# Moving the attention denominators of a four-layer block: eleven under x^T k, five under the outputs, and key sums in half rows

## The chip, the cores and the metric

The kernel runs on one core of one Trainium2 chip. The metric is the device time of one execution in microseconds (us), as the median of several executions. A step of 2% would be 33 us; everything below is about single microseconds, so the argument rests on the traces, in which stretches repeat to 0.01 us, and the medians only confirm it. Blocks marked as profile show chosen lines of a view; "..." marks lines left out (in the prediction's blocks they are left out without a mark).

## The reference

Four layers with residuals: linear attention (A), a gated feed-forward (B), A, B, on x of 2048 x 1024.

```python
def _A_ref(x, wqkv, wo):                 # 32 heads of 32
    ...                                  # q, k, v from x @ wqkv
    phi = lambda t: jnp.where(t > 0, t + 1, jnp.exp(t)) + 1e-6
    pq, pk = phi(q), phi(k)
    kv  = jnp.einsum("bhsd,bhse->bhde", pk, v)
    z   = jnp.einsum("bhsd->bhd", pk)                      # the key sum
    num = jnp.einsum("bhqd,bhde->bhqe", pq, kv)
    den = jnp.einsum("bhqd,bhd->bhq", pq, z)[..., None] + 1e-6   # the denominators
    o = num / den
    return (...o...) @ wo

x = x + _A_ref(_layernorm(x), A_wqkv, A_wo)
x = x + _B_ref(_layernorm(x), B_W_gate, B_W_up, B_W_down)
...                                      # and both once more
```

## The kernel before

The kernel works in 16 blocks of 128 rows, in four quarters of four blocks. In an attention layer TensorE first projects k and q with phi on the other engines, then forms x^T k for the whole sequence (the "x^T k phase", 16 units of 16 matmuls), then projects the last quarter of q, folds kv into the output weights (16 fold matmuls), and computes the outputs. TensorE writes each result into a buffer of its accumulator memory, PSUM, and can reuse the buffer only when VectorE or ScalarE has read it; copying a result out is called its evacuation. The denominators, one per block and head, must be applied to the phi of q before its transpose goes to the outputs. Three parts per block: a product on GpSimd, a sum and a reciprocal on VectorE, a scaling on GpSimd; then a transposing DMA.

```python
def z_mult(sc, j):
    prod = self.prodp.tile([P, D], F32, tag="prod")        # one buffer
    nc.gpsimd.tensor_tensor(out=prod, in0=pq_of[sc, j], in1=zrow, op=ALU.mult)
    later.at(2, lambda: z_sum(prod, sc, j))

def z_sum(prod, sc, j):
    den = self.small.tile([P, D // HD], F32, tag="den")
    nc.vector.tensor_reduce(out=den, in_=heads(prod), ...)
    nc.vector.tensor_scalar(out=den, in0=den, scalar1=1e-6, ...)
    nc.vector.reciprocal(out=den, in_=den)
    later.at(2, lambda: z_scale(den, sc, j))

def z_scale(den, sc, j):
    nc.gpsimd.tensor_tensor(out=heads(pq), in0=heads(pq), in1=den..., op=ALU.mult)
    ...
    nc.sync.dma_start_transpose(out=pqT[sc][:, :, j * P:(j + 1) * P], in_=pq)
```

`later.at(n, f)` calls f after n further steps; a step is one unit of eight matmuls. It places an instruction in the program of its engine. The engines themselves are only held by the semaphores of the data. In the order in which they stand in the source: the phi of one unit on ScalarE and VectorE, the evacuation of a fold, and the schedule.

```python
nc.scalar.activation(out=e, in_=ps, func=ACT.Exp)                     # phi, form "v"
nc.vector.tensor_scalar(out=e, in0=e, scalar1=1.0, scalar2=1e-6,      # L305
                        op0=ALU.min, op1=ALU.add)
nc.vector.scalar_tensor_tensor(out=out, in0=ps, scalar=0.0, in1=e,    # L316
                               op0=ALU.max, op1=ALU.add)
...
if g % 2:                                                             # a fold's PSUM tile
    nc.scalar.activation(out=dst, in_=ps, func=ACT.Copy)
else:
    nc.vector.tensor_copy(out=dst, in_=ps)                            # L466
...
later.at(ZR, z_row)                                # the key sum, spread over all partitions
for i in range(self.ST - QT):
    later.at(ZR + 2 + i * 5 // 2, lambda i=i: z_mult(*divmod(i, QT)))
for d in range(KT):
    m_units(d)                                     # the x^T k phase
...
run(q3[:3])                                        # last quarter's q, then with folds
run([with_fold(u, i) for i, u in enumerate(q3[3:] + out0[:3])])
...
for j in range(QT):
    later.at(1 + Z3 * j, lambda j=j: z_mult(self.NQ - 1, j))
run(out0[3:])
```

Of the kernel before, what the change touches and what calls it, by code (L numbers as in the profile page):

```python
# [7 lines left out]
ALU = mybir.AluOpType  # L8
# [5 lines left out]
NW = 512  # L14
HD = 32
QT = 4
LNLAG = 1
ZR = 5
Z3 = 3
PHILAG = 2  # L20
KINDS = (("vvss", "vvss"), ("vvss", "vvss"))
# [62 lines left out]
class _Net:  # L84
# [255 lines left out]
    def layer_A(self, l, last_ln):  # L340
        nc, G, KT, D = self.nc, self.G, self.KT, self.D
        ring, later = self.ring, self.later
        H = D // NW
# [5 lines left out]
        ksum = self.prodp.tile([P, D], F32, tag="prod", name=f"ksum{l}")  # L349

        def project(name, l_q, j):
            w = ring.get((l, name))
            ps = self.ps.tile([P, NW], F32, tag="a")
            for kt in range(KT):
                nc.tensor.matmul(ps, lhsT=self.xnT[l, l_q][:, kt, j * P:(j + 1) * P],  # L355
                                 rhs=w[:, kt, :], start=(kt == 0), stop=(kt == KT - 1))
            return ps

        def k_unit(q, j, c):
            t = q * QT + j  # L360
            pk = self.pk_home(l, t)
            self.phi(project(f"k{c}", q, j), pk[:, c * NW:(c + 1) * NW], KINDS[l // 2][min(q, 1)][c])
            if c == H - 1:
                later.at(1 + self.phi_lag, lambda: k_sum(t))

        def k_sum(t):
            pk = self.pk_home(l, t)
            if t == 0:
                nc.gpsimd.tensor_copy(out=ksum, in_=pk)  # L369
            else:  # L370
                nc.gpsimd.tensor_tensor(out=ksum, in0=ksum, in1=pk, op=ALU.add)  # L371

        def z_row():

# [9 lines left out]
        def m_units(d):  # L384
            mt = self.ep.tile([P, D], BF16, tag="e", name=f"mt{l}_{d}")
            for h in range(H):
                ps = self.ps3.tile([P, NW], F32, tag="b")
                for t in range(self.ST):
                    nc.tensor.matmul(ps, lhsT=self.xn[l, t][:, d * P:(d + 1) * P],  # L389
                                     rhs=self.pk[l, t][:, h * NW:(h + 1) * NW],  # L390
                                     start=(t == 0), stop=(t == self.ST - 1))
                    if t == self.ST // 2 - 1:
                        later.tick()
                nc.scalar.activation(out=mt[:, h * NW:(h + 1) * NW], in_=ps, func=ACT.Copy)
                if h == H - 1:
                    later.at(2, lambda: kv_step(d, mt))
                later.tick()
# [35 lines left out]
        def z_mult(sc, j):  # L433
            prod = self.prodp.tile([P, D], F32, tag="prod")
# [5 lines that stand above are left out]
            nc.vector.tensor_reduce(out=den, in_=heads(prod), axis=mybir.AxisListType.X, op=ALU.add)  # L440
            nc.vector.tensor_scalar(out=den, in0=den, scalar1=1e-6, scalar2=None, op0=ALU.add)
            nc.vector.reciprocal(out=den, in_=den)  # L442
            later.at(2, lambda: z_scale(den, sc, j))
# [10 lines left out]
        def fold_wo(i):  # L454
            n2, g = divmod(i, G)
            if n2 == 0 and g % 2 == 0:
                T.append(self.slab.tile([P, 2, D], BF16, tag="slab", name=f"T{l}_{g // 2}"))
            pool, tag = (self.kvp, f"kv{g // 2 % 2}") if g % 2 else (self.ps3, "b")
            ps = pool.tile([P, NW], F32, tag=tag, name=f"fold{l}_{i}")
            nc.tensor.matmul(ps, lhsT=kvT[:, g, :], rhs=ring.get((l, f"o{n2}"))[:, g, :],  # L460
                             start=True, stop=True)
            dst = T[g // 2][:, g % 2, n2 * NW:(n2 + 1) * NW]
            if g % 2:
# [3 lines that stand above are left out]
# [16 lines left out]
        def column_major(f, q):  # L483
            return [lambda j=j, c=c: f(q, j, c) for c in range(H) for j in range(QT)]

        def row_major(f, q):
            return [lambda j=j, c=c: f(q, j, c) for j in range(QT) for c in range(H)]

        def run(*lists):

            n = max(len(u) for u in lists)
            for i in range(n):
                for u in lists:
                    if i < len(u):
                        u[i]()
                        later.tick()
# [5 lines left out]
        for i in range(QT, self.ST):  # L502
            self.ln_at((4 if l == 0 else 2) + 3 * (i - QT), l, i, 2)
        first = column_major(k_unit, 0)
        if l == 0:

# [16 lines left out]
        for q in range(1, self.NQ - 1):  # L523
            run(row_major(k_unit, q), row_major(q_unit, q))
        run(row_major(k_unit, self.NQ - 1))
        with self.tc.manual_schedule(engines={mybir.EngineType.DVE, mybir.EngineType.Pool}):
            ring.free_before((l, "v0"))
            later.at(ZR, z_row)
            for i in range(self.ST - QT):
                later.at(ZR + 2 + i * 5 // 2, lambda i=i: z_mult(*divmod(i, QT)))  # L530
            for d in range(KT):
                m_units(d)
            if l > 0:
                later.at(1, lambda: [self.bring_back(t) for t in range(self.NS)])
            q3 = row_major(q_unit, self.NQ - 1)
            out0 = column_major(out_unit, 0)

            def with_fold(u, i):
                return lambda: (u(), fold_wo(2 * i), fold_wo(2 * i + 1))

            run(q3[:3])
            run([with_fold(u, i) for i, u in enumerate(q3[3:] + out0[:3])])
            ring.free_slowly((l, "o0"), later, 2)
            for j in range(QT):
                later.at(1 + Z3 * j, lambda j=j: z_mult(self.NQ - 1, j))
            run(out0[3:])
            self.ln_later(last_ln, 0, 5, 4, 3)
            for sc in range(1, self.NQ):
                run(row_major(out_unit, sc))
# [132 lines left out]
```

## Time and profile before

The kernel before took 1641.26 us (median of the runs). Its trace, from the starts of TensorE's instructions in the timeline:

| stretch | us | of it lost |
|---|---|---|
| fourth group of transposes to the first x^T k matmul, first layer (17.94 to 109.37) | 91.43 | 1.8 |
| first last-quarter matmul to the next layer, first attention layer (168.18 to 244.15) | 75.97 | 3.0 |
| the same, second attention layer (979.82 to 1055.78) | 75.96 | 3.0 |

The prediction read the ends of the last stretch from another view, each 0.16 later; the length is the same. I shall call the first stretch the *first quarter* (its waits all lie there) and the others the *fold stretch*. The lines of the page, of the waits and of the fold stretch are in the prediction. For the first quarter, these are lines of VectorE and GpSimd from the timeline (start, length, line, operation, tiles, shapes; in brackets what the engine waited for):

```profile
21.13 0.85 DVE L305 TENSOR_SCALAR e<-e 128x512 f32<-128x512 f32 x1 [0.53 <-ACT e L304]
...
26.83 2.03 DVE L305 TENSOR_SCALAR e<-e 128x512 f32<-128x512 f32 x1 [0.53 <-ACT e L304]
28.78 0.68 DVE L316 SCALAR_TENSOR_TENSOR slab<-ps,e 128x512 bf16<-128x512 f32 x1
...
20.67 1.04 POOL L369 CAST ksum<-slab 128x1024 f32<-128x1024 bf16 x1 [19.36 <-DVE slab L316]
24.13 4.44 POOL L371 TENSOR_TENSOR ksum<-ksum,slab 128x1024 f32<-128x1024 f32 x2 [2.42 <-DVE slab L316]
```

Two whole-row key sums stand back to back from 24.13 on; the L305 that starts at 26.83 ends only 0.3 us after them, and the L316 behind it frees the PSUM buffer that TensorE waits for until 29.51. The first sum, at 20.67, stretches the L305 of 21.13 to 0.85.

### The profile page before, as it was taken

How to read it: one execution, taken by the hardware profiler on the slowest of the kernel's cores; microseconds unless marked ns; L12 is line 12 of the kernel's file. 1: busy time of each engine (PE TensorE's matmuls, PEld its weight loads, DVE VectorE, ACT ScalarE, POOL GpSimd, SP SyncE). 2: the span in 40 equal slices, each digit the busy share in tenths (PEclk: the TensorE clock that was granted, in tenths of full speed). 3: DMA queues.
4: the chain of work that ended last, by engine and by line, in shares of the span. 5: the costliest groups of instructions: out<-in, count | busy, mean ns of one | idle time of the engine just before them, and what ended most of it. 6: DMA issues, size and time to landing. Idle time of an engine off the chain costs nothing.

```text
span 1639.1 us, 18247 instructions
## 1 busy us (share of the span) xinstructions
PE 1617.8 (99%) x7506; PEld 742.7 (45%) x7658; DVE 576.8 (35%) x947; ACT 332.6 (20%) x635; POOL 194.7 (12%) x102
## 2 busy tenths in 40 slices
PE   8999999999999999999999999999999999999999
PEld 3444444444444444444444444444444444444444
DVE  7854686122212321222165548842121112211111
ACT  5741202101110110111067312121011101101110
POOL 1249220000000000000023574100000000000000
PEclk9999999999999999999999999999999999999999
DMA  8313537458445544544550148374544464455442
GB/s 252 57 52 59 173 65 177 149 167 238 155 138 171 179 151 158 160 151 138 168 129 1 58 102 237 72 199 145 176 150 150 158 197 153 141 162 161 155 160 71
DMA packets 298244, 235.04 MB, mean 143 GB/s; under 512 B 101296, under 2 KB 294192, under 8 KB 298160
## 3 DMA queue, kind: packets, MB, share of 16 engines
q1 hardware_dynamic: 293408, 229.66, 47.5%
q10 hardware_dynamic: 4752, 4.20, 0.8%
q8 instruction: 60, 0.98, 0.3%
q14 instruction: 24, 0.20, 0.0%
HBM read 201.33 MB, written 8.39 MB: 128 GB/s over the span
## 4 chain that ended last, share of the span: by engine, by line
PE 83%; DVE 1%; issue 1%; ACT 0%; ACTq 0%
PE acc L605 23%; PE pu L581 23%; PE pg L581 23%; PE ps L355 6%; PE ps L389 3%; PE ps L472 3%; PE acc_last L605 0%; DVE e L305 0%; PE kv L402 0%; DVE T L466 0%; DVE den L440 0%; DVE pq L316 0%; PE fold L460 0%; DVE kvT L414 0%; DVE den L442 0%
## 5 line engine op out<-in xcount | busy, mean ns | idle before, releaser
L581 PEld LDWEIGHTS <-t 128*128 128x128 bf16 x3584 | 350.7, 98 | 422.8
L581 PE MATMUL pu<-xnT,t 128*128 128x512 bf16 x1757 | 420.2, 379 | 1.9
L581 PE MATMUL pg<-xnT,t 128*128 128x512 bf16 x1756 | 419.8, 379 | 1.8
L605 PE MATMUL acc<-t,hT 128*128 128x512 bf16 x1727 | 380.6, 379 | 1.9
L587 DVE TENSOR_TENSOR hT<-pu,rg 128x512 bf16<-128x512 f32 x224 | 154.7, 691 | 572.7 <-PE pu L581 553.3
L586 ACT ACTIVATE rg<-pg 128x512 f32<-128x512 f32 x224 | 133.5, 596 | 737.0 <-PE pg L581 665.5
L605 PEld LDWEIGHTS <-hT 128*128 128x128 bf16 x1820 | 178.1, 98 | 209.0
L355 PE MATMUL ps<-t,xnT 128*128 128x512 bf16 x1002 | 223.0, 379 | 4.2 <-DVE slab L316 1.3
L355 PEld LDWEIGHTS <-xnT 128*128 128x128 bf16 x1024 | 99.8, 98 | 123.5 <-issue 3.2
L472 PE MATMUL ps<-T,pqT 128*128 128x512 bf16 x502 | 111.6, 379 | 1.1 <-DVE T L466 0.6
L154 ACT ACTIVATE rstd<-mv,eps 128x1 f32<-128x1 f32 x64 | 18.8, 294 | 332.4 <-DVE mv L152 332.4
L622 DVE TENSOR_TENSOR xo<-x,acc 128x512 bf16<-128x512 f32 x31 | 21.3, 687 | 170.3 <-PE acc L605 170.3
L147 DVE BATCH_NORM_STATS2 stats<-x 128x6 f32<-128x512 f32 (+1 forms) x120 | 78.1, 672 | 0.8
L472 PEld LDWEIGHTS <-pqT 128*128 128x128 bf16 x512 | 50.1, 98 | 61.3 <-issue 1.1
L435 POOL TENSOR_TENSOR prod<-pq,zrow 128x1024 f32<-128x1024 bf16 x32 | 68.3, 2134 | 72.0 <-DVE den L440 61.2
L369 POOL CAST ksum<-x 128x1024 f32<-128x1024 bf16 x1 | 1.0, 1037 | 621.5 <-DVE x L316 621.5
L619 DVE TENSOR_TENSOR x<-x,acc 128x512 f32<-128x512 f32 x32 | 21.6, 674 | 138.5 <-PE acc L605 137.4
L316 DVE SCALAR_TENSOR_TENSOR pq<-ps,e 128x512 bf16<-128x512 f32 x64 | 43.9, 687 | 57.9 <-ACT e L311 57.3
L447 POOL TENSOR_TENSOR pq<-pq,den 128x1024 bf16<-128x1024 bf16 x32 | 61.5, 1923 | 13.0 <-DVE den L442 13.0
L371 POOL TENSOR_TENSOR ksum<-ksum,slab 128x1024 f32<-128x1024 f32 x23 | 49.2, 2140 | 86.8 <-DVE slab L316 76.8
L305 DVE TENSOR_SCALAR e<-e 128x512 f32<-128x512 f32 x80 | 49.2, 615 | 28.5 <-ACT e L304 28.4
L440 DVE TENSOR_REDUCE den<-prod 128x32 f32<-128x1024 f32 x32 | 38.9, 1216 | 49.9 <-POOL prod L435 49.9
(58 smaller groups left out, 619.5 us busy)
## 6 DMA issues: line engine op xcount, KB each, us to landing
t<-in_B_W_gate_dram SPq DMA_DIRECT2D x56, 1024.0 KB, 6.7
t<-in_B_W_up_dram SPq DMA_DIRECT2D x56, 1024.0 KB, 5.2
t<-in_B_W_down_dram SPq DMA_DIRECT2D x64, 896.0 KB, 5.0
t<-in_A_wqkv_dram SPq DMA_DIRECT2D x11, 1024.0 KB, 6.1
t<-in_A_wo_dram SPq DMA_DIRECT2D x4, 1024.0 KB, 7.4
away<-x SPq DMA_DIRECT2D x8, 512.0 KB, 3.9
x<-away SPq DMA_DIRECT2D x8, 512.0 KB, 8.5
out_dram<-xo ACTq DMA_DIRECT2D x31, 128.0 KB, 2.1
```

Of the source, the lines that this page charges most:

```text
L147: self.nc.vector.bn_stats(out=stats[:, c, :], in_=src[:, c * fmax:(c + 1) * fmax])
L305: nc.vector.tensor_scalar(out=e, in0=e, scalar1=1.0, scalar2=1e-6, op0=ALU.min, op1=ALU.add)
L355: nc.tensor.matmul(ps, lhsT=self.xnT[l, l_q][:, kt, j * P:(j + 1) * P], rhs=w[:, kt, :], start=(kt == 0), stop=(kt == KT - 1))
L371: nc.gpsimd.tensor_tensor(out=ksum, in0=ksum, in1=pk, op=ALU.add)
L389: nc.tensor.matmul(ps, lhsT=self.xn[l, t][:, d * P:(d + 1) * P], rhs=self.pk[l, t][:, h * NW:(h + 1) * NW], start=(t == 0), stop=(t == sel ...
L435: nc.gpsimd.tensor_tensor(out=prod, in0=pq_of[sc, j], in1=zrow, op=ALU.mult)
L447: nc.gpsimd.tensor_tensor(out=heads(pq), in0=heads(pq), in1=den[:, :].unsqueeze(2).to_broadcast([P, D // HD, HD]), op=ALU.mult)
L472: nc.tensor.matmul(ps, lhsT=pqT[sc][:, g, j * P:(j + 1) * P], rhs=T[g // 2][:, g % 2, n2 * NW:(n2 + 1) * NW], start=(g == 0), stop=(g == G ...
L581: nc.tensor.matmul(ps, lhsT=w[:, kt, fi * P:(fi + 1) * P], rhs=self.xnT[l, q][:, kt, :], start=(kt == 0), stop=(kt == KT - 1))
L586: nc.scalar.activation(out=rg, in_=pg, func=ACT.Relu)
L587: nc.vector.tensor_tensor(out=h[:, fi, :], in0=pu, in1=rg, op=ALU.mult)
L605: nc.tensor.matmul(ps[:, 0:n], lhsT=hT[ft // 4][:, ft % 4, j * P:(j + 1) * P], rhs=wd[:, k, i * n:(i + 1) * n], start=(ft == 0), stop=(ft ...
```

## The change

The intent: take the last denominators of the x^T k phase out of the last quarter's phi and folds, by placing one block fewer there and the others closer together; and let the key sums block the phi for shorter times, by halving them, and in the first quarter not at all, by placing them later.

```diff
+NZ = 11
...
-            if c == H - 1:
-                later.at(1 + self.phi_lag, lambda: k_sum(t))
-        def k_sum(t):
-            pk = self.pk_home(l, t)
+            later.at(1 + (10 if self.phi_lag else 0), lambda: k_sum(t, slice(c * NW, (c + 1) * NW)))
+        def k_sum(t, cols):
+            pk = self.pk_home(l, t)[:, cols]
             if t == 0:
-                nc.gpsimd.tensor_copy(out=ksum, in_=pk)
+                nc.gpsimd.tensor_copy(out=ksum[:, cols], in_=pk)
...
-            for i in range(self.ST - QT):
-                later.at(ZR + 2 + i * 5 // 2, lambda i=i: z_mult(*divmod(i, QT)))
+            for i in range(NZ):
+                later.at(ZR + 2 + 2 * i, lambda i=i: z_mult(*divmod(i, QT)))
...
-            for j in range(QT):
-                later.at(1 + Z3 * j, lambda j=j: z_mult(self.NQ - 1, j))
+            for i in range(NZ, self.ST):
+                later.at(1 + Z3 * (i - NZ), lambda i=i: z_mult(*divmod(i, QT)))
```

`phi_lag` is 2 in the first quarter of the first layer and 0 elsewhere. All line numbers after the constants are one higher in the changed kernel: L305 becomes L306, L316 L317, L466 L467, L472 L473.

More of the change, by code (lines that the diff above doesn't have):

```diff
@@ L362, in k_unit @@
             self.phi(project(f"k{c}", q, j), pk[:, c * NW:(c + 1) * NW], KINDS[l // 2][min(q, 1)][c])
-            if c == H - 1:
-                later.at(1 + self.phi_lag, lambda: k_sum(t))
-        def k_sum(t):
-            pk = self.pk_home(l, t)
+            later.at(1 + (10 if self.phi_lag else 0), lambda: k_sum(t, slice(c * NW, (c + 1) * NW)))
+        def k_sum(t, cols):
+            pk = self.pk_home(l, t)[:, cols]
             if t == 0:
-                nc.gpsimd.tensor_copy(out=ksum, in_=pk)
+                nc.gpsimd.tensor_copy(out=ksum[:, cols], in_=pk)
             else:
-                nc.gpsimd.tensor_tensor(out=ksum, in0=ksum, in1=pk, op=ALU.add)
+                nc.gpsimd.tensor_tensor(out=ksum[:, cols], in0=ksum[:, cols], in1=pk, op=ALU.add)
         def z_row():
```

## The prediction

> **What bounds the kernel now.** The page comes first: TensorE (PE) is busy in 99% of the span at full granted clock in every slice, and the chain that ended last is 83% PE.
>
> ```profile
> span 1639.1 us, 18247 instructions
> PE 1617.8 (99%) x7506; PEld 742.7 (45%) x7658; DVE 576.8 (35%) x947; ACT 332.6 (20%) x635; POOL 194.7 (12%) x102
> ```
>
> So a change that leaves every matmul in place can gain only what PE stands idle, and the next view is the list of waits, read for PE alone (us in total, times, longest):
>
> ```profile
> PE fold L460 <- DVE T L466: 4.5, 4, 1.2
> PE ps L355 <- DVE slab L316: 1.3, 1, 1.3
> PE ps L472 <- DVE T L466: 0.6, 2, 0.3
> PE ps L355 <- DVE pq L316: 0.3, 1, 0.3
> ```
>
> The rest of PE's idle time lies before 12 us, at the load of the first blocks, where the change does nothing. The fold waits occur twice in each attention layer. The timeline of VectorE (DVE) and GpSimd (POOL) of the first such place shows why (start, length, line, shapes):
>
> ```profile
> 174.12 1.21 DVE L440 TENSOR_REDUCE den<-prod 128x32 f32<-128x1024 f32 x1
> 175.85 1.97 DVE L305 TENSOR_SCALAR e<-e 128x512 f32<-128x512 f32 x1
> 178.46 1.41 DVE L305 TENSOR_SCALAR e<-e 128x512 f32<-128x512 f32 x1
> 180.51 0.68 DVE L466 CAST T<-fold 128x512 bf16<-128x512 f32 x1
> ...
> 175.41 2.12 POOL L435 TENSOR_TENSOR prod<-pq,zrow 128x1024 f32<-128x1024 bf16 x1 [12.78 <-DVE den L440]
> 177.49 2.10 POOL L447 TENSOR_TENSOR pq<-pq,den 128x1024 bf16<-128x1024 bf16 x1
> ```
>
> Two denominators' sums fall among the last quarter's phi and the folds, and the GpSimd work behind them stretches L305 from 0.42 to 1.97 us. The fold's evacuation (L466) comes late, its two PSUM buffers are full, and PE waits.
>
> I size the loss by start-to-start times. In long stretches 49 matmuls take 10.74 us and a 0.05 us step follows: 10.79 / 50 = 0.216 us each. From the first last-quarter matmul (168.18) to the first of the next layer (244.15) are 75.97 us. In it are 64 projection, 16 fold and 256 output matmuls, 336 x 0.216 = 72.5, and a kv step of 0.45: 72.95. **Lost: 3.0 us**, and the second layer (979.98 to 1055.94) gives the same, so 6.0 in all. In the first quarter the same method adds the pipelined tail of about 0.16 to each listed idle: 1.27 + 0.28 becomes 1.43 + 0.44 = 1.9 us.
>
> **What the Trainium skill says.** "Perfetto Trace Analysis", Identifying the Most-Contended Engine: matmul busy time does not measure nearness to roofline. I use it here only to find the gaps, and the weight loads' 45% agrees that 99% says little else. "SBUF — State Buffer", Who interferes with whom: GpSimd shares a port pair with VectorE; a VectorE instruction in a 2-port mode (tensor_scalar among them) and a GpSimd instruction exclude each other for their full length, the later one blocking. The trace agrees: the L305 at 175.85 ends at 177.82, just after the product that began at 175.41, and the scale after it is stretched from 1.91 to 2.10; so the one that has waited goes next, even between two GpSimd instructions. L316 and L466, with a PSUM operand, keep their 0.69 and 0.68. "GPSIMD Engine Reference", Elementwise: a two-input add is bound by GpSimd's one read port, and measured 4497 ns for 2048 columns, 2.2 ns a column. The 2.13 us of L371 for 1024 columns, 2.1 ns a column, agrees; so I estimate 1.07 us for half a row, plus a dispatch that no run here shows apart.
>
> **The change part by part.**
>
> *Eleven blocks in the x^T k phase.* Before, twelve products are placed there 2.5 steps apart, so the sums of blocks 10 and 11 are placed behind the phi of the last quarter (steps 34 and 36 of a phase of 32). But steps only set the order on each engine: GpSimd runs back to back at 2.12 + 1.91, measured 3.95 us from product to product, from 123.10 to 162.6. With 2 steps, the product of block 10 is at step 27, its sum at 29, its scale at 31, all ahead of the last quarter. The order is also changed: product 2 comes before scale 0, and must wait for sum 1 on the single product buffer, an opening of 1.3 us. So: product 2 at 126.5, product 3 at 130.5, product 10 at 130.5 + 7 x 3.95 = 158.1, scale 10 done at about 166. Product 11 has no input left to wait for and follows at 166 to 168, before the first last-quarter L305 at 170.80. Then GpSimd is idle until the sum of block 11, behind the fourth output unit or later.
>
> With that, on VectorE per last-quarter unit: 0.42 + 0.69 phi + 0.68 evacuation, with overlaps 1.73 us, against 2 x 0.216 + 1.73 = 2.16 on PE. The first fold's evacuation moves from 180.5 to about 177.5 (the unit's e is ready at 176.39, then 1.05 of phi); the fold that needs its buffer is due at 179.85. There is 1.7 us of slack there and about as much at each later one. All 3.0 us go, in both layers: **-6.0 us**.
>
> *Five blocks under the outputs.* One product, sum and scale more, 3 steps apart. The last scale ends at 220.6 before; one place later is 3 x 1.73 = 5.2 us, less 2.5 to 3 for the earlier start: about 223. Its transpose lands 3.1 us later, 226. The output unit that reads block 15 is the second last pair, at about 244.15 - 3.0 - 3.5 = 237.6. Eleven us of slack, so **0**. VectorE has 3 x 0.69 + 1.74 = 3.8 us of work per 5.2 us there; the layernorm that starts at 212 may be held by one more GpSimd pair, while four PSUM buffers give PE about 5 us.
>
> *Half rows.* 32 instead of 16 instructions a layer, 34 us of GpSimd time unchanged, in a stretch where it is a third busy. From 70 to 98 us L305 comes every 3.45 us just behind a full row; halves end earlier. In the k-only last eight units halves may block each L305 by 0.6, inside the buffers' slack. The last sum ends near 113 instead of 114.25, but PE reaches the matmul that needs it at 118.0 in its own order. **0**.
>
> *Held back in the first quarter.* The step is 11 instead of 3. But a step is only a place in an engine's program, and GpSimd has nothing else in its program there. That it runs ahead of its step the trace shows: block 12's product is placed after the fourth output unit's matmuls (about 194) and ran at 184.93, when its buffer came free. In the quarter, the sums start 0.06 to 0.15 us after the join they need (20.61 to 20.67, 30.51 to 30.66). So I expect the hold to hold nothing, and the halves to start earlier than the full rows did, at 14.9. Followed by hand: the half of block 1 is ready at 17.45, queues behind the L163 of 17.34 and then blocks the L305 of 17.85 for about 0.9 us; the next halves catch the L305 at 23.5 and that at 28.5. The join that PE waits for at 29.5 (28.78 to 29.46) comes to about 30.0: **+0.5 us**, and ScalarE's dense row from there to 43.8 carries it on. If a few tenths fall otherwise, the long block of L305 at 26.83 (2.03) halves and 0.9 is won.
>
> Sum: -6.0 + 0 + 0 + 0.5 = -5.5; 1641.4 - 5.5 = 1635.9.
>
> **The rivals.** (1) The hold does act as its name says: no lock in the first quarter, L305 at 26.83 takes 0.42, and its 1.9 us go too: 1641.4 - 6.0 - 1.9 = 1633.5. The early block-12 product speaks against it. (2) The folds keep a wait: GpSimd is late by the 1.3 us opening and more, so that product 11 reaches into the last quarter, or the evacuations stay late because kvT (1.28 us) and the phi alone fill VectorE. Half of the gain would be left: about 1639. Against it: 2.7 us between 168 and 170.8, and VectorE's 11.69 us idle before it. (3) The wait moves: the fifth late block delays layernorm or the transposes that the next layer's first matmul needs, and PE waits at 244. That costs 1 to 3 us a layer: 1638 to 1641. Against it: PE shows no wait there, the layernorm of the last block stands seven steps behind the last sum. (4) The early locks of the first quarter cost more, up to 1.5 us: 1637.
>
> **Range and chances.** Weights: my sum or near it 0.5, rival 1 0.2, rival 4 0.15, rivals 2 and 3 0.15. I put the number at 1635.8 and the range at 1633.3 to 1639.0. 2% is 32.8 us; PE's whole idle time in the span is 1639.1 - 1617.8 = 21.3 us, so faster by over 2% is out of reach, and nothing here adds a matmul or a transfer.
>
> **What would show each step.** Right: no wait of the fold or of the first output unit on L466; all last-quarter L305 near 0.42; GpSimd without an instruction from 168 until the sum of block 11; 73.0 us from the first last-quarter matmul to the next layer, in both layers; no wait at the next layer's start. Half sums of about 1.07 us, the first at about 14.9 in spite of the hold. The hold works if the first half comes after 27 us. The prediction is wrong if the stretch is still above 74 us, if a wait of PE on L316 between 24 and 44 us sums to over 3 us or vanishes, or if the k phases of either layer show a new wait.

## The result

The changed kernel took 1635.49 us (median of 4, 1634.67 to 1635.94), the kernel before 1641.26 (median of 4, 1640.76 to 1641.49). The ratio is 0.9965, with a 95% interval of 0.9947 to 0.9982. Here and below a ratio is the mean time of one kernel's fast runs over that of the other's in the same rounds, so it is not quite the ratio of the medians.

From the changed kernel's page its span and its engines' busy times, then its list of TensorE's waits (us in total, times, longest), without the first line, a wait of 2.1 us before any data has come, which is the same in all profiles:

```profile
span 1634.0 us, 18308 instructions
...
PE 1616.6 (99%) x7506; PEld 742.7 (45%) x7658; DVE 571.6 (35%) x947; ACT 331.9 (20%) x635; POOL 201.8 (12%) x134
```

```profile
PE ps L356 <- DVE slab L317: 1.4, 4, 0.4
PE ps L356 <- DVE xnT L262: 1.3, 2, 1.0
PE ps L356 <- DMA t<-in_A_wqkv_dram: 1.3, 1, 1.3
PE ps L356 <- DVE pq L317: 0.3, 1, 0.3
```

The waits on the folds' evacuation are gone. The one wait of 1.3 us on the phi's last step (L316 in the kernel before) has become four of 0.3 to 0.4. The two waits on xnT and on the first weights lie before 12 us; they vary from profile to profile with the arrival of the first data (the wait for the weights is 0.5 us in the profile before and between nothing and 1.3 in the others) and belong to no part of the change.

The fold stretch of the first layer, VectorE and GpSimd:

```profile
175.52 0.43 DVE L306 TENSOR_SCALAR e<-e 128x512 f32<-128x512 f32 x1 [0.49 <-ACT e L305]
...
177.25 0.43 DVE L306 TENSOR_SCALAR e<-e 128x512 f32<-128x512 f32 x1 [0.57 <-ACT e L305]
...
178.31 0.68 DVE L467 CAST T<-fold 128x512 bf16<-128x512 f32 x1
...
161.03 5.66 POOL L448 TENSOR_TENSOR pq<-pq,den 128x1024 bf16<-128x1024 bf16 x3
166.64 2.13 POOL L436 TENSOR_TENSOR prod<-pq,zrow 128x1024 f32<-128x1024 bf16 x1
199.17 2.13 POOL L436 TENSOR_TENSOR prod<-pq,zrow 128x1024 f32<-128x1024 bf16 x1 [30.40 <-DVE den L441]
```

The last scales of the phase end at 166.69, product 11 at 168.77, and GpSimd then does nothing until 199.17. The phi's L306 take 0.43 us and VectorE waits for ScalarE between them. The first quarter, the same two engines:

```profile
18.20 1.33 DVE L306 TENSOR_SCALAR e<-e 128x512 f32<-128x512 f32 x1
...
23.79 1.37 DVE L306 TENSOR_SCALAR e<-e 128x512 f32<-128x512 f32 x1
...
28.61 1.06 DVE L306 TENSOR_SCALAR e<-e 128x512 f32<-128x512 f32 x1 [0.53 <-ACT e L305]
29.59 0.68 DVE L317 SCALAR_TENSOR_TENSOR slab<-ps,e 128x512 bf16<-128x512 f32 x1
...
15.19 0.61 POOL L370 CAST ksum<-slab 128x512 f32<-128x512 bf16 x1 [13.89 <-DVE slab L317]
17.80 1.45 POOL L372 TENSOR_TENSOR ksum<-ksum,slab 128x512 f32<-128x512 f32 x1 [2.00 <-DVE slab L317]
```

The sums "held back" start at 15.19, 5.5 us earlier than the whole rows did, each as soon as its half is joined. Three L306 are stretched, by 0.90, 0.94 and 0.63 us, instead of two by 1.6 and 0.4: 2.5 us in all instead of 2.0, and the stretch is longer by as much.

The account, by stretches of TensorE (starts from the timelines):

| kernel | first quarter | fold stretch, layers 1 and 2 | median, us |
|---|---|---|---|
| before | 91.43 | 75.97, 75.96 | 1641.26 |
| changed | 91.89 | 72.97, 72.97 | 1635.49 |
| difference | +0.46 | -3.00, -2.99 | -5.77 |

The three stretches sum to -5.53. The profiled spans differ by 5.1 (1639.1 to 1634.0): in the changed kernel's profile the fourth group of transposes stands 0.36 later (18.30 against 17.94), by the waits before 12 us, and this is the rest. The medians differ by 0.24 more than the stretches, which is within the spread of the runs.

### The profile page after: what moved, and what is told of

Same layout as the page of the kernel before. It is cut to its first block, busy times and chain, and to the rows that moved or that the text cites. A ratio compares the mean times of both kernels' runs of the same rounds, so it can differ in the third digit from the quotient of the medians.

```text
span 1634.0 us, 18308 instructions
## 1 busy us (share of the span) xinstructions
PE 1616.6 (99%) x7506; PEld 742.7 (45%) x7658; DVE 571.6 (35%) x947; ACT 331.9 (20%) x635; POOL 201.8 (12%) x134
## 4 chain that ended last, share of the span: by engine, by line
PE 97%; DVE 1%; ACT 1%; issue 1%; DMA 0%; SPq 0%
PE pu L582 24%; PE pg L582 24%; PE acc L606 23%; PE ps L356 12%; PE ps L473 7%; PE ps L390 7%; PE kv L403 0%; PE fold L461 0%; DMA t<-in_A_wqkv_dram 0%; PE acc_last L606 0%; DVE e L306 0%; DVE stats L148 0%; DVE slab L317 0%; ACT e L310 0%; DVE st L148 0%
## 5 line engine op out<-in xcount | busy, mean ns | idle before, releaser
L473 PE MATMUL ps<-T,pqT 128*128 128x512 bf16 x502 | 111.3, 379 | 0.5
L473 PEld LDWEIGHTS <-pqT 128*128 128x128 bf16 x512 | 50.1, 98 | 60.4
L372 POOL TENSOR_TENSOR ksum<-ksum,slab 128x512 f32<-128x512 f32 x46 | 54.2, 1184 | 84.9 <-DVE slab L317 75.3
L317 DVE SCALAR_TENSOR_TENSOR pq<-ps,e 128x512 bf16<-128x512 f32 x64 | 43.9, 688 | 58.6 <-ACT e L312 58.0
L390 PE MATMUL ps<-slab,x 128*128 128x512 bf16 x250 | 56.1, 379 | 0.3
```

Source lines behind the costliest of these rows:

```text
L372: nc.gpsimd.tensor_tensor(out=ksum[:, cols], in0=ksum[:, cols], in1=pk, op=ALU.add)
L390: nc.tensor.matmul(ps, lhsT=self.xn[l, t][:, d * P:(d + 1) * P], rhs=self.pk[l, t][:, h * NW:(h + 1) * NW], start=(t == 0), stop=(t == sel ...
L473: nc.tensor.matmul(ps, lhsT=pqT[sc][:, g, j * P:(j + 1) * P], rhs=T[g // 2][:, g % 2, n2 * NW:(n2 + 1) * NW], start=(g == 0), stop=(g == G ...
```

## The experiments

The theory is that of the prediction: the folds are relieved because the last sums stand ahead of the last quarter's phi; the hold does nothing; half rows without a real hold cost half a microsecond. Each kernel below is the changed kernel with one edit, runs beside the kernel before on the same chip, and gave correct outputs. In the three sessions of runs, the kernel before took 1640.81, 1640.91 and 1640.74.

### Without the hold

```diff
-later.at(1 + (10 if self.phi_lag else 0), lambda: k_sum(...))
+later.at(1 + self.phi_lag, lambda: k_sum(...))
```

> The changed kernel without the hold: key sums placed 3 steps behind their projection in the first quarter instead of 11; half rows kept. Theory (the hold holds nothing, since a step only sets the order on GpSimd, which has nothing else there): the first half sum again at about 15.2 us, each at the same distance from its join, from the fourth group of transposes to the first x^T k matmul 91.9 us as in the changed kernel, and the time within 0.3 us of it, about 1635.5. Rival (the hold does keep sums away from the phi): sums start earlier than in the changed kernel, more L306 are blocked, and the first quarter loses another 0.5 to 1.5 us: 1636 to 1637.

Measured: 1635.42 us (5 runs), ratio to before 0.9966. First quarter 91.90, fold stretch 72.96 in both layers. GpSimd's first lines:

```profile
14.32 0.61 POOL L370 CAST ksum<-slab 128x512 f32<-128x512 bf16 x1 [13.01 <-DVE slab L317]
16.93 1.45 POOL L372 TENSOR_TENSOR ksum<-ksum,slab 128x512 f32<-128x512 f32 x1 [2.00 <-DVE slab L317]
```

The fourth group of transposes is at 17.43 here and at 18.30 in the changed kernel, so the first half stands 3.11 us ahead of it in both. The later sums of the quarter agree in the same way, to 0.01 us. The rival falls: the hold changes no start at all. (I had written "about 15.2"; the 0.87 us between that and 14.32 is only the shift of the whole trace.)

### Whole rows, no hold: the denominators' move alone

```diff
-later.at(1 + (10 if self.phi_lag else 0), lambda: k_sum(t, slice(c * NW, (c + 1) * NW)))
+if c == H - 1:
+    later.at(1 + self.phi_lag, lambda: k_sum(t, slice(0, D)))
```

> The changed kernel with the key sums as before: whole rows, 3 steps behind. Only the move of the denominators is left of the change. Theory (half rows cost 0.5 us in the first quarter and bring nothing): 91.4 us from the fourth group of transposes to the first x^T k matmul, as in the kernel before, one wait of about 1.3 us of the projections on the phi's last step instead of four of 0.3 to 0.4, the stretch of folds and outputs 73.0 us in both layers: about 1635.0. Rival (half rows are part of the gain): slower than the changed kernel, up to 1636.5.

Measured: 1635.07 us (5 runs), ratio 0.9965. First quarter 91.43 as in the kernel before, with its one wait of 1.27 us back; fold stretch 72.97 in both layers. So the move of the denominators carries all of the gain, and the half rows cost 0.46 us of the first quarter. The medians agree in sign (0.35 under the run above), though their ranges overlap.

### Twelve blocks, 2 steps apart

```diff
-NZ = 11
+NZ = 12
```

> The changed kernel with twelve blocks in the x^T k phase, 2 steps apart, and four under the outputs as before. Theory (what counts is that the last sum stands ahead of the last quarter's phi, not the number of blocks): product 11 follows the scales at about 166.6, its sum is at step 31, its scale ends at about 171.5, no L306 of the last quarter above 0.6 us or so, no wait on the folds, 73.0 us from the first last-quarter matmul to the next layer in both layers, about 1635.5. Rival (GpSimd is full there and twelve do not fit, so the fifth block had to go under the outputs): the first L306 of the last quarter are blocked by up to 2 us, the folds wait again, 74 us or more in each layer, 1637.5 or more.

Measured: 1635.11 us (5 runs), ratio 0.9966; fold stretch 72.97 in both layers, no wait on a fold. The twelve scales end at 169.94. One thing I had not seen: with product 11 out of the way, the product of block 12, whose phi is the first of the last quarter, finds the buffer free and goes ahead of its place into the last quarter:

```profile
174.40 2.12 POOL L436 TENSOR_TENSOR prod<-pq,zrow 128x1024 f32<-128x1024 bf16 x1 [4.46 <-DVE pq L317]
...
174.82 1.99 DVE L306 TENSOR_SCALAR e<-e 128x512 f32<-128x512 f32 x1 [0.49 <-ACT e L305]
```

So one L306 took 1.99, against my 0.6, and TensorE still did not wait. The number of blocks is not what counts.

### Eleven blocks, 2.5 steps apart

```diff
-later.at(ZR + 2 + 2 * i, ...)
+later.at(ZR + 2 + i * 5 // 2, ...)
```

> The changed kernel with its eleven blocks, but 2.5 steps apart as before. Product 10 is then at step 32, its sum at step 34, behind the second last-quarter phi, and the scale of 10 and product 11 follow it on GpSimd. Theory (each sum among the phi costs VectorE 1.7 us and the GpSimd pair behind it stretches one or two L306; there was room for about one such pair but not for two): the sum at about 174, one or two L306 stretched to 1.4 us and more, the fold waits 0 to 0.8 us a layer instead of 3.0, 73.0 to 73.8 us a layer, 1635.5 to 1637. Rival (the loss is proportional to the sums left): half of it stays, 74.5 us a layer, 1638.5.

Measured: 1635.42 us (4 runs), ratio 0.9967; fold stretch 72.97 in both layers. The sum of block 10 is back among the phi and two L306 are stretched, yet no wait is left:

```profile
174.46 1.21 DVE L441 TENSOR_REDUCE den<-prod 128x32 f32<-128x1024 f32 x1
...
177.19 1.42 DVE L306 TENSOR_SCALAR e<-e 128x512 f32<-128x512 f32 x1
...
179.85 1.02 DVE L306 TENSOR_SCALAR e<-e 128x512 f32<-128x512 f32 x1
```

The loss is not proportional to the sums left: one is free, two cost all of the 3.0 us.

### Twelve blocks, 2.5 steps apart

Both edits of the two experiments before together, key sums as in the changed kernel.

> The changed kernel with both halves of the move undone: twelve blocks, 2.5 steps apart; the key sums stay as in the changed kernel. Theory (in the kernel before, two sums of 1.73 us and 3.5 us of stretched L306 came to 7.0 us of extra VectorE time among the last quarter, of which 4.0 found room and 3.0 did not; with eleven blocks or with 2 steps the extra is 3.3 or 1.6 and all fits): the sums of 10 and 11 are back among the phi, the fold waits return, 75.9 to 76.0 us a layer in both layers, and the time is that of the changed kernel plus 6.0, about 1641.4, a little above the kernel before because of the half rows. Rival (half rows contribute to the folds' relief): less than 75.5 us a layer.

Measured: 1641.28 us (4 runs) beside 1640.74, ratio 1.0002; fold stretch 75.97 in both layers, first quarter 91.90. The list of waits has the folds again:

```profile
PE fold L461 <- DVE T L467: 4.5, 4, 1.2
```

The three runs together say: fewer blocks or closer places, either is enough, and with neither the loss is back in full. The half rows have no part in it. An accounting that fits, though no run isolates its terms: the kernel before has two sums of 1.73 us (174.12 to 175.85) and four L305 stretched by 1.55, 0.99, 0.40 and 0.61 in the last quarter, 7.0 us of extra VectorE time. If 3.0 of it reached TensorE, 4.0 was absorbed by the two PSUM buffers and VectorE's gaps; the extra was 1.73 + 1.0 + 0.6 = 3.3 in the run with eleven wide blocks and 1.57 in that with twelve close ones, both under 4.0.

### A real hold

The sums of the first quarter are put behind a tiny GpSimd copy that reads the phi of the third query unit and writes two elements of the sum, which the first real copies then overwrite. GpSimd works in order, so all eight halves wait for that phi.

```diff
-later.at(1 + (10 if self.phi_lag else 0), lambda: k_sum(...))
+if not self.phi_lag:
+    later.at(1, lambda: k_sum(t, slice(c * NW, (c + 1) * NW)))
+elif t == 0 and c == 0:
+    later.at(14, held)
+
+def held():
+    nc.gpsimd.tensor_copy(out=ksum[:, :].rearrange("p (c n) -> p c n", c=H)[:, :, 0:1],
+                          in_=pq_of[0, 2][:, 0:H].unsqueeze(2))
+    for t in range(QT):
+        for c in range(H):
+            k_sum(t, slice(c * NW, (c + 1) * NW))
```

> The changed kernel with a real hold: all eight half sums of the first quarter stand behind a tiny GpSimd copy into the sum that reads the phi of the third query unit (ready at about 34 us), so they cannot start earlier; the copy's values are overwritten. Theory (the first quarter's loss is the port: GpSimd sums blocking L306): no GpSimd sum before 34 us, every L306 between 14 and 30 us near 0.42 us, no wait of a projection on the phi's last step before 40 us; ScalarE's row from 27 to 44 us then leaves at most 0.5 us of wait. 89.5 to 90 us from the fourth group of transposes to the first x^T k matmul instead of 91.9: about 1633.4, faster than both kernels. Rival (the quarter is bound by ScalarE's phi and layernorm anyway): the wait moves to about 44 us and 91.4 or more remains: 1635 or more.

Measured: **1632.95 us** (5 runs, 1632.30 to 1633.08), ratio to before 0.9951, interval 0.9937 to 0.9964. This beats both kernels. The first quarter takes 89.62 us:

```profile
33.25 0.19 POOL L370 CAST ksum<-pq 128x2 f32<-128x2 bf16 x1 [31.95 <-DVE pq L317]
33.49 1.16 POOL L380 CAST ksum<-slab 128x512 f32<-128x512 bf16 x2
34.62 6.92 POOL L382 TENSOR_TENSOR ksum<-ksum,slab 128x512 f32<-128x512 f32 x6
...
26.35 0.43 DVE L306 TENSOR_SCALAR e<-e 128x512 f32<-128x512 f32 x1 [0.53 <-ACT e L305]
...
18.26 31.91 PE L356 MATMUL ps<-t,xnT 128*128 128x512 bf16 x146
```

No sum before 33.49, every L306 before that near 0.43, and TensorE's projections stand in one piece where the changed kernel has six. The wait that remained to be feared, ScalarE's row up to 44 us, did not come. So the time at which GpSimd's sums run is the whole cause of the 2.3 us that the changed kernel loses in the first quarter (91.89 - 89.62): moving them, and nothing else, removes it. That they act by blocking L306 is seen in its lengths, 0.41 to 0.43 us here against up to 1.37; that the shared port is the reason is the prediction's reading, with which this agrees.

### A real hold with whole rows

The same hold, but `k_sum(t, slice(0, D))` for whole blocks, in all quarters.

> The kernel with the real hold, but whole rows everywhere: four whole-row sums of the first quarter behind the tiny copy, whole rows in all other quarters. Theory (half rows bring nothing once the sums are held): 89.6 us from the fourth group of transposes to the first x^T k matmul, no wait on the phi, 1632.95 within 0.4. Rival (halves are needed because a whole row blocks a phi or a layernorm for twice as long): waits of 0.5 us or more between 34 and 60 us, 1633.5 or more.

Measured: 1633.88 us (5 runs), ratio 0.9956. First quarter 90.16, that is 0.54 more than with halves; my theory for this run was wrong. The layernorm's scaling, which is also a tensor_scalar in SBUF, runs while the held sums run; first with halves, then with whole rows:

```profile
36.90 1.39 DVE L164 TENSOR_SCALAR x<-x,mv,rstd 128x1024 bf16<-128x1024 bf16 x1
```

```profile
37.29 2.35 DVE L164 TENSOR_SCALAR x<-x,mv,rstd 128x1024 bf16<-128x1024 bf16 x1
...
42.74 65.77 PE L356 MATMUL ps<-t,xnT 128*128 128x512 bf16 x304 [0.56 <-DVE pq L317]
```

Undisturbed, L164 takes 0.54. It was held 0.85 us by a half and 1.8 by a whole row, and the phi of q behind it came late for TensorE by 0.56. Half rows are of use after all, but only under a hold that holds: alone they cost 0.46, with it they save 0.54.

### The five late blocks further apart

```diff
-Z3 = 3
+Z3 = 5        # in a second run: 4
```

> The changed kernel with the five blocks under the outputs 5 steps apart instead of 3. The last scale then comes 4 x 2 x 1.73 = 13.8 us later, at about 237.5 instead of 223.7, and its transpose lands about 3.1 us after that, at 240.6; the output units of block 15 begin at 238.5. Theory (the slack under the outputs is about 11 to 12 us and nothing else hangs on it): PE waits 2 to 3 us for the transposed query block in each layer, about 75.3 us instead of 73.0, 1640. Rival (the blocks under the outputs gate nothing at this distance): 73.0 and 1635.5. If a layernorm or the next layer's first matmul is what waits, the wait appears at the next layer's start instead.

Measured: 1642.74 us (4 runs), ratio 1.0009; fold stretch 78.37 and 76.49, so 5.4 and 3.5 us longer instead of 2 to 3. The last scale of the first layer ends at 239.10. The waits of TensorE:

```profile
PE pu L582 <- DMA xnT<-xn: 4.5, 2, 2.8
...
PE ps L473 <- DMA pqT<-pq: 0.7, 1, 0.7
```

Slack does run out, but mostly elsewhere than I had said. TensorE waits 0.7 us for the transposed query block, in the second layer alone, and 4.5 in the two layers for the transposed input of the next layer. In this build four of the next layer's matmuls stand before the last two output units in TensorE's program (a compiled order, not a choice of the kernel), and they wait, in the first layer, for a layernorm block whose transpose was issued at 237.36 and took 4.02 us to land:

```profile
241.51 1.86 PE L582 MATMUL pu<-xnT,t 128*128 128x512 bf16 x4 [2.83 <-DMA xnT<-xn]
...
1053.50 1.02 PE L582 MATMUL pu<-xnT,t 128*128 128x512 bf16 x4 [1.64 <-DMA xnT<-xn]
```

The waits are not all of the 5.4 and 3.5 us. In each layer 0.86 us is no loss: the four early matmuls are work of the next layer that this build counts into the stretch. In the first layer about 1.6 us more came after the wait: the four matmuls took 1.86 us and not 1.02, because the granted clock was 0.50 from 242 to 244 us, and 1.00 again from 245 on. Three of the four runs show a mean clock of 0.999, the fourth 1.0, and that one took 1641.58 us, 1.0 to 1.4 less than the others. After the shorter wait of the second layer the matmuls kept their pace. So about 4.5 and 2.7 us are lost; their sum, 7.2, is what the medians show (1642.74 - 1635.49 = 7.25). How much of the wait is the program order and how much the crowding of VectorE and of the transposes, this run cannot tell.

> The changed kernel with the five late blocks 4 steps apart instead of 3. The last scale comes 4 x 1.73 = 6.9 us later, at about 230.6, its transpose lands at about 234, before the output units of block 15 at 238.5. Theory (5 steps were past the slack, 4 are inside it): 73.0 us a layer, 1635.4. Rival (what made 5 steps slow is the order on TensorE, in which the build puts a few of the next layer's matmuls ahead of the last output units, or the next layer's transposes queued behind the late ones): the same waits, smaller, at the next layer's start: 73.5 us or more.

Measured: 1635.37 us (4 runs), ratio 0.9967; fold stretch 72.97 in both layers, and no wait on either. Its last scale ends at 231.39. So the slack of the late blocks, with all that hangs on them, ends somewhere between 4 and 5 steps, that is for a last scale between 231.4 and 239.1; the changed kernel, with 223.66, is at least 7.7 us inside it.

## Why the prediction was right

The number was 1635.8 and the measured median 1635.49; step by step:

- **The fold stretch, -6.0.** Measured -3.00 and -2.99. The rate of 0.216 us a matmul gave 72.95 for the stretch without waits, and 72.97 was measured. The run with only this part of the change has the same two stretches, and the one with both halves of it undone has 75.97 again. The step was right, and so were its times on GpSimd: product 10 at 158.96 and the last scale at 166.69 against 158.1 and 166, and nearly all of the difference is the 0.8 us by which this trace runs later there.
- **What the step did not say.** It reads as if both the closer places and the block fewer were needed. Either alone suffices; by the accounting above, about 4 us of extra VectorE time is absorbed. The prediction had the slack of 1.7 us per fold but did not ask how much disturbance it would bear.
- **Five blocks under the outputs, 0.** Right: the last scale ended at 223.66 against "about 223", and there was no wait. The reason given, 11 us of slack to the output units, was not tested cleanly: past the slack, most of the wait was for the next layer's input, the place that rival 3 had named. At 3 steps, as predicted, rival 3 did not come.
- **Half rows, 0 outside the first quarter.** Right for TensorE, with no new wait in any k phase. The size was off: the median half took 1.16 us and not 1.07, so GpSimd's time was not unchanged; it rose from 194.7 to 201.8 us.
- **The hold holds nothing, +0.5.** Right. The first half came at 15.19, that is 14.8 without the 0.36 us shift, against 14.9; the blocked L306 were those followed by hand (18.20, 23.79, 28.61); the first quarter lost 0.46 more. The run without the hold shows the starts unmoved, and the run with a real hold shows that rival 1's mechanism was sound and only its cause absent: with the sums really late, 89.62 us, so 1.8 less than the kernel before, against the 1.9 the rival put on it. One reading behind this step was loose: block 12's product ran at 184.93 not because its buffer came free then (the sum of block 11, which had read that buffer last, ended at 182.32) but because scale 11, from 183.06 to 184.97, stands before it on GpSimd; it was ahead of its step all the same.
- **The alternative of a 0.9 us gain** from the L305 at 26.83 did not come: that L306 was stretched by 0.63 instead of 1.6, but two earlier ones had made the whole row late by then.
- **Rivals 2 and 4** fell: no fold wait was left, and the early locks cost 0.46, not up to 1.5.

## What to carry to other kernels

A position in a program is not a time: an engine with nothing else queued runs an instruction as soon as its data is there, and what held it back here was a data dependence (a two-element copy). When GpSimd and VectorE share the port, ask which VectorE instruction each GpSimd instruction will meet, and give the moved work a place where that instruction has slack; splitting it shortens each block but makes more of them, which cost 0.46 us among the first phi and saved 0.54 under the real hold. Size a wait by start-to-start times against the count of matmuls, and expect buffers to absorb some disturbance: here one denominator's sum among the phi cost nothing, and two cost 3.0 us a layer. A wait can cost more than its length: behind one of 2.83 us the granted clock was 0.50 for some 3 us.

## What the Trainium skill lacked or had wrong

- "GPSIMD Engine Reference", Instruction dispatch, puts the software dispatch at tens of cycles and gives no time for a whole elementwise instruction's fixed cost. By the reported lengths two half-row sums take 2 x 1.155 us and a whole row 2.13, so about 0.18 us per instruction would be fixed. By their starts under the real hold, halves come every 1.11 us (34.62, 35.73, 36.85) and whole rows, which each wait for the one before, every 2.21 (35.02, 37.23, 39.44), so back to back the halves cost next to nothing more. The whole change added 7.1 us of reported GpSimd time with 32 more instructions, part of it stretching.
- "SBUF — State Buffer", Who interferes with whom, says that whichever starts first gets the port and the other blocks, not what happens when GpSimd has its next instruction ready too. In the kernel before, the L305 that had waited since 175.85 went between two back-to-back GpSimd instructions (it took 1.97 us, and the scale after it 2.10 instead of 1.91).
- "Perfetto Trace Analysis", GPSIMD Engine Instruction, calls GpSimd's reported spans unreliable. Here they could be used for two-input operations to within 4%: product and scale were reported as 2.12 + 1.91 = 4.03 us, and came every 3.95; half-row sums were reported as 1.16, and came every 1.11.
